# An expert layer's row gathers: half rows fetched by GpSimd against whole rows fetched by GpSimd and dealt out on chip by SyncE

## The chip, the core and the metric

The kernel runs on one core of a Trainium2 chip. The core has five engines with instruction lists of their own: TensorE (PE in the profile; PEld is its weight load), VectorE (DVE), ScalarE (ACT), GpSimd (POOL) and SyncE (SP), which here only issues transfers. They meet through semaphores. The metric is the device time of one execution in microseconds; less is better.

## The reference, cut to what matters

```python
def reference(x, w_r, w_i, b_r, b_i, moe):       # x: 8 x 1856 x 256
    X = np.fft.rfft(x, axis=1)
    Yr = soft_threshold(Xr @ w_r - Xi @ w_i + b_r, 0.01)
    Yi = soft_threshold(Xr @ w_i + Xi @ w_r + b_i, 0.01)
    y = np.fft.irfft(Yr + 1j * Yi, n=1856, axis=1)   # 14848 rows of 256
    # each row goes to one of 4 groups, and in it to one of 4 experts (argmax)
    for g, e in all 16 experts:
        h = np.maximum(y[rows of g, e] @ w1[g, e], 0)        # 256 x 1024
        out[rows of g, e] = (gate of the row) * (h @ w2[g, e])   # 1024 x 256
```

## The kernel before

The front part (transforms, threshold and routing, up to about 430 us) follows a long written order and isn't touched. It leaves the transformed rows y in DRAM as `ys_d` (one row of 256 floats, 1 KB, each) and for each expert a list of row numbers and gates in DRAM, `lst`.

The main part is a loop over 40 jobs. A job is up to 432 rows of one expert, in tiles of 128. Four experts ("fixed": 3, 1, 2 and 0) come at places known when the kernel is written; the other twelve come in the order of their size ("ranks" 0 to 11), which SyncE reads at run time from `order_r`. Ranks 1 to 9 have three jobs each, with the row counts in `CUTS`. The first four jobs fetch and transpose their rows on TensorE (`fetch`, `prep`). Jobs 4 to 39 are dealt:

- `deal` (from line 565) fills a tile `xm` (128 partitions x 4 tiles x 2 x 128 floats). It gathers half rows: for each tile and each half `b_` of its 128 rows one indirect transfer of 128 pieces of 512 B, by `half_ids`, row numbers doubled and arranged by eight small GpSimd computations for each 32-partition piece (L562). Partitions 64a to 64a+31 then hold the first halves of 32 rows, and the next 32 partitions their second halves.
- `turn_rows` transposes `xm` on VectorE in four instructions (L583) into `xtf`, and ScalarE and VectorE split that into two parts, `xth` (L589) and `xtl` (L590), whose sum keeps full accuracy in TensorE's fast format.
- `up_g` multiplies with w1 (L620, six matmuls for each of eight blocks), ScalarE takes the ReLU (`hh`, L625), VectorE the remainder (`hl`, L627).
- `down_g` multiplies with w2 (L693, L694), ScalarE and VectorE apply the gate (L698, L699; four buffers `yo`), and `store` sends each tile to its rows of `out` by an indirect transfer of GpSimd (L667).
- A new expert's weights come as two loads of 1 MB on SyncE into two buffers `xt` (L515), followed by the lists of its rows (L1105, L1107), in `dma_next`. `split_w` splits them piece by piece on ScalarE (L527) and VectorE (L528); the second load waits until a buffer has been split.

In iteration i the program is written in this order: down of job i-1 (two tiles), index computations of a new expert, `deal` of job i+2, up of job i with the pieces of a weight split, the loads of the next expert, `turn_rows` of job i+1, the rest of down of job i-1. GpSimd's list follows the program (`manual_schedule`); the other engines' lists are set by a scheduler.

Of the kernel before, what the change touches and what calls it, by code (L numbers as in the profile page):

```python
# [9 lines left out]
F32 = mybir.dt.float32  # L10
F32R = mybir.dt.float32r
BF16 = mybir.dt.bfloat16
I32 = mybir.dt.int32
AF = mybir.ActivationFunctionType
ALU = mybir.AluOpType
# [3 lines left out]
NB, S, D = 8, 1856, 256  # L19
# [5 lines left out]
NPAD = NP * PAIR  # L25
# [111 lines left out]
def spectral_moe(ctx: ExitStack, tc: tile.TileContext, x, wri, bri, wgate, w1, w1q, w2, cst, out):  # L137
    nc = tc.nc
# [6 lines left out]
    ys_d = dram.tile([NPAD + 1, D], F32, name="ys_d")  # L145
# [206 lines left out]
    def indices(ids, pool, both=True):  # L352
        if both:
            nc.gpsimd.tensor_copy(out=ids.gi, in_=ids.ent[:, :, 0])
        tmp = pool.tile([128, 12], F32, name="ixt", bufs=1)[:, 0:ids.n]
        nc.gpsimd.tensor_scalar(out=tmp, in0=ids.ent[:, :, 0], scalar1=0.0, scalar2=float(NPAD + 1), op0=ALU.is_equal, op1=ALU.mult)
        nc.gpsimd.tensor_scalar_add(out=tmp, in0=tmp, scalar1=-1.0)
        nc.gpsimd.tensor_tensor(out=tmp, in0=tmp, in1=ids.ent[:, :, 0], op=ALU.add)
        nc.gpsimd.tensor_copy(out=ids.si, in_=tmp)

    class Ids:
        def __init__(self, ent, gi, si):
            self.ent, self.gi, self.si, self.n, self.last = ent, gi, si, gi.shape[1], 128
            self.half = None

        def cut(self, a_, b_):
            part = Ids(self.ent[:, a_:b_], self.gi[:, a_:b_], self.si[:, a_:b_])
            if self.half is not None:
                part.half = self.half[:, a_:b_]
            if b_ == self.n:  # L370
                part.last = self.last
            return part
# [131 lines left out]
    with tc.issue_after(x1.ins):  # L504
        nc.sync.dma_start(out=lst[0:NE * CAP].rearrange("(e s) k -> e s k", e=NE)[:, 0:ZROWS].rearrange("e (j c) k -> e j (c k)", j=16),
                          in_=zero[0:NE, 0:ZROWS // 16].rearrange("p c k -> p (c k)").unsqueeze(1).broadcast_to([NE, 16, ZROWS // 8]))
# [44 lines left out]
            out_.append((xg, w, ids.rows(c0 + w - 1)))  # L551
        return out_

    half_rows = ys_d.rearrange("r (h d) -> (r h) d", h=2)

    def half_ids(ids, nm):
        ids.half = ft.tile([128, ids.n, 2], I32, name=f"half_{nm}")
        for a_ in range(2):
            for b_ in range(2):
                for h in range(2):  # L560
                    q, p = 64 * a_ + 32 * h, 64 * b_ + 32 * a_
                    nc.gpsimd.tensor_scalar(out=ids.half[q:q + 32, :, b_], in0=ids.ent[p:p + 32, :, 0], scalar1=2.0, scalar2=float(h),  # L562
                                            op0=ALU.mult, op1=ALU.add)

    def deal(ids):
        xm = xq.tile([128, 4, 2, 128], F32, name="xm")
        for c in range(ids.n):
            for b_ in range(2):
                left = ids.rows(c) - 64 * b_
                if left > 0:  # L570
                    m = 64 if left <= 32 else 128
                    nc.gpsimd.indirect_dma_start(  # L572
                        out=xm[0:m, c, b_, :], out_offset=None, in_=half_rows,
                        in_offset=bass.IndirectOffsetOnAxis(ap=ids.half[0:m, c, b_:b_ + 1], axis=0))
        return xm.rearrange("p c b d -> p (c b) d")

    def turn_rows(xm, ids):
# [516 lines left out]
    first, xp2 = [], None  # L1094
# [43 lines left out]
    by_hand = ExitStack()  # L1138
# [16 lines left out]
        assert not (sorts or moved or turns or parked) and all(next(g, None) is None for c, g in steps.items() if c not in "SNOP")  # L1155
        wts = {e: views(w) for e, w in wts.items()}
    inv.close()
    by_hand.enter_context(tc.manual_schedule(engines={mybir.EngineType.Pool}))

    xq = ctx.enter_context(tc.tile_pool(name="xq", bufs=2, reuse_waits="tile"))  # L1160
    hq = ctx.enter_context(tc.tile_pool(name="hq", bufs=2, reuse_waits="tile"))
# [201 lines left out]
    def ranked(k):  # L1363
        return nc.values_load(order_r[:, k:k + 1], engines=sp, min_val=0, max_val=NE - 1)

    def halves(parts, ids):
        c = 0
        for p in parts:
            p.half = ids.half[:, c:c + p.n]
            c += p.n  # L1370
        return parts

    def rank_ids(k, ek):
        rows = CUTS[k]
        n = sum((m + 127) // 128 for m in rows)
# [56 lines left out]
    def dma_next(i):  # L1432
        if not loads:
            return
        j = loads.pop(0)
        kind, q = jobs[j]
        if kind == "l":
            raws[j] = raw_w(q[0], w1q)
        else:
            k = q[0]  # L1440
            ek = ranked(k)
            raws[j] = raw_w(ek, w1q)
            rids[k], whole = rank_ids(k, ek)
            ready[i + 2] = lambda: (indices(whole, ft), half_ids(whole, f"r{k}"), halves(rids[k], whole))

    table = flex_table()
    for j, (kind, q) in enumerate(jobs):
# [11 lines left out]
            indices(fids[e][0], ft, False)  # L1459

    ready[0] = fixed_ids
    ready[3] = lambda: (half_ids(fids[0][0], "f0"), halves(fids[0][1], fids[0][0]))
    for i, (kind, q) in enumerate(jobs):
        ids = jids[i]
        if kind == "r":
# [49 lines left out]
    next(rest)  # L1515
    drain(behind_)
    drain(rest)
    by_hand.close()

    nfx = nc.values_load(nflex[:, 0:1], min_val=0, max_val=128)  # L1520
    with tc.For_i(KF, nfx, 1) as iv:
        rw, ids = flex_load(bass.ds(iv, 1))
        wt, todo = split_w(rw)
        emit(todo, len(todo))
        hts, hs = [], h_tiles()
        drain(flex_mm(prep(xq, fetch(xp2, ids, 3), 128), wt, hts))
        for q in range(2):
            flex_tr(hts[q], q, hs)
        down(psy, "py", hs, ids, wt, None, range(1))
        wt, ids = half_load(bass.ds(iv, 1))  # L1530
        hts, h = [], hq.tile([128, 8, WIDE], F32, name="hh")
        drain(half_mm(half_prep(fetch(xp2, ids, 3)), wt, hts))
        for q in range(2):
            half_tr(hts[q], q, h)
        half_down(h, ids, wt, None)
# [40 lines left out]
```

## Time and profile before

| what | value |
|---|---|
| median of 3 runs | 1128.2 us (1123.73 to 1131.09) |
| the profiled execution | 1122.3 us, span 1120.4 us |
| mean granted TensorE clock | 0.972 |
| TensorE busy | 1044.0 us (93%) |
| VectorE, ScalarE, GpSimd busy | 742.5, 486.4, 539.8 us |

The span runs from the first to the last instruction; the execution's time has 1.9 us around it. Times in the trace count from the span's start. "PEclk" is the TensorE clock granted, 1.00 being 2.4 GHz. SyncE's issuing of transfers is not counted as busy time.

### The profile page before, as it was taken

The page shows a single profiled execution, that of the slowest core. Times are in us where ns is not written, and L with a number is a line of the kernel's source. Part 1 is how long each engine was busy: PE and PEld are TensorE (multiplying, and loading weights), DVE is VectorE, ACT ScalarE, POOL GpSimd, SP SyncE. Part 2 cuts the span into 40 slices and gives each one's busy share as a digit, 9 for nine tenths or more (in the row PEclk, how much of TensorE's full clock was granted, in tenths as well). Part 3 has the DMA queues.
Part 4 walks back from the last instruction along what each step waited for, and adds up shares of the span by engine and source line. Part 5 has one row for each costly group of instructions (what it writes and reads, how often), then busy time and mean ns, then how long its engine had stood idle before and what let it go on. Part 6 is the DMA issues. An engine that isn't in the chain of part 4 may idle for free.

```text
span 1120.4 us, 24666 instructions
## 1 busy us (share of the span) xinstructions
PE 1044.0 (93%) x9496; PEld 897.6 (80%) x9496; DVE 742.5 (66%) x1754; ACT 486.4 (43%) x1273; POOL 539.8 (48%) x792
## 2 busy tenths in 40 slices
PE   8999999999999989898997999989899999997996
PEld 4886767767768878897896988878798888986896
DVE  6879999999897744462664757465575666655552
ACT  2664546437544333251443445243453544433442
POOL 0210255463764685644364554655365664463722
PEclk9999999999999999998998999999899999998989
DMA  9403314404135212312322223131322322223100
GB/s 386 120 2 131 135 40 153 151 5 153 49 127 183 81 58 58 123 64 75 100 80 88 85 69 117 42 126 45 104 85 70 128 65 94 78 86 98 48 30 28
DMA packets 34698, 105.32 MB, mean 94 GB/s; under 512 B 15052, under 2 KB 15769, under 8 KB 28050
## 3 DMA queue, kind: packets, MB, share of 16 engines
q1 hardware_dynamic: 16338, 55.92, 14.4%
q0 software_dynamic: 13344, 30.79, 9.2%
q10 hardware_dynamic: 4896, 17.01, 3.9%
q8 instruction: 76, 1.25, 0.5%
q14 instruction: 44, 0.36, 0.1%
HBM read 71.37 MB, written 32.46 MB: 93 GB/s over the span
## 4 chain that ended last, share of the span: by engine, by line
PE 62%; DVE 15%; issue 10%; POOL 6%; ACT 3%; DMA 3%; another core or an unknown queue 2%; ACTq 0%; POOLq 0%; SPq 0%; DVEq 0%
PE ph L620 21%; PE py L693 9%; PE py L694 5%; PE pw L885 5%; PE py L715 5%; PE ph L1045 3%; PE pw L867 2%; PE bank L909 2%; DMA big<-in_x_dram 2%; PE bank L927 2%; PE bank L803 2%; POOL xm L572 2%; PE bank L438 2%; POOL out_dram L667 1%
## 5 line engine op out<-in xcount | busy, mean ns | idle before, releaser
L620 PE MATMUL ph<-xth,big 128*128 128x256 f32 (+8 forms) x1280 | 298.1, 316 | 17.1 <-DVE hl L627 8.5
L627 DVE SCALAR_TENSOR_TENSOR hl<-ph,hh 128x256 fp32r<-128x256 f32 (+8 forms) x528 | 169.3, 355 | 176.2 <-ACT hh L625 110.9
L625 ACT ACTIVATE hh<-ph 128x256 fp32r<-128x256 f32 (+8 forms) x528 | 152.5, 337 | 222.6 <-PE ph L620 141.7
L620 PEld LDWEIGHTS ph<-xth,big 128*128 128x128 f32 x1280 | 220.4, 191 | 23.3 <-issue 12.5
L693 PE MATMUL py<-big,hh 128*128 128x512 f32 (+2 forms) x608 | 223.6, 405 | 8.3 <-ACT hh L625 4.4
L572 POOL DMA_INDIRECT xm<-ys_d,half_r x176 | 172.7, 981 | 68.3 <-issue 48.2
L620 PE MATMUL ph<-xtl,big 128*128 128x256 f32 (+8 forms) x640 | 201.6, 315 | 3.3 <-DVE xtl L590 2.9
L667 POOL DMA_INDIRECT out_dram<-yo,si_r x92 | 93.0, 1011 | 210.2 <-DVE yo L699 174.7
L694 PE MATMUL py<-big,hl 128*128 128x256 f32 (+2 forms) x608 | 175.3, 288 | 3.8 <-DVE hl L627 2.2
L693 PEld LDWEIGHTS py<-big,hh 128*128 128x128 f32 (+2 forms) x608 | 116.0, 191 | 37.2 <-ACT hh L625 6.2
L620 PEld LDWEIGHTS ph<-xtl,big 128*128 128x128 f32 x640 | 122.3, 191 | 6.3 <-DVE xtl L590 4.9
L694 PEld LDWEIGHTS py<-big,hl 128*128 128x128 f32 (+2 forms) x608 | 115.9, 191 | 9.6 <-DVE hl L627 6.5
L715 PE MATMUL py<-hh,big 128*128 128x320 f32 (+4 forms) x320 | 79.4, 327 | 9.0 <-issue 8.6
L851 POOL TENSOR_TENSOR xdl<-xd,xdh 128x512 fp32r<-128x512 f32 (+1 forms) x23 | 28.0, 1219 | 108.4 <-ACT xdh L844 88.1
L583 DVE STREAM_TRANSPOSE xtf<-xm 64x384 f32<-64x384 f32 (+3 forms) x144 | 72.8, 506 | 1.5
L589 ACT CAST xth<-xtf 128x512 fp32r<-128x512 f32 (+5 forms) x59 | 28.4, 517 | 101.4 <-DVE xtf L583 93.1
L528 DVE TENSOR_TENSOR big<-xt,big 128x512 fp32r<-128x512 f32 x104 | 70.9, 682 | 0.9 <-issue 0.2
L885 PE MATMUL pw<-wh,xh 128*128 128x256 f32 x240 | 66.5, 299 | 2.8 <-DVE pw L875 2.6
L715 PEld LDWEIGHTS py<-hh,big 128*128 128x128 f32 x320 | 57.9, 199 | 9.9 <-issue 8.4
L527 ACT CAST big<-xt 128x512 fp32r<-128x512 f32 x104 | 65.3, 627 | 0.0
L885 PE MATMUL pw<-wl,xh 128*128 128x256 f32 x240 | 62.0, 280 | 0.0
L890 ACT ACTIVATE big<-pw,nlam 128x512 f32<-128x512 f32 x60 | 41.4, 690 | 46.6 <-PE pw L885 45.7
(265 smaller groups left out, 2021.6 us busy)
## 6 DMA issues: line engine op xcount, KB each, us to landing
xt<-in_w_dram SPq DMA_DIRECT2D x21, 1024.0 KB
ys_d<-ysb ACTq DMA_DIRECT2D x32, 512.0 KB
xt<-in_w1q_dram SPq DMA_DIRECT2D x13, 1024.0 KB
big<-in_x_dram SPq DMA_DIRECT2D x8, 1024.0 KB
xt<-in_x_dram SPq DMA_DIRECT2D x8, 1024.0 KB
xm<-ys_d,half_r POOLq DMA_INDIRECT x176
out_dram<-yo,si_r POOLq DMA_INDIRECT x92
CI<-in_cst_dram SPq DMA_DIRECT2D x1, 1088.0 KB
```

The source lines that it names most:

```text
L527: nc.scalar.copy(out=wt[:, 2 * i, cs], in_=raws[i][:, cs])
L528: nc.vector.tensor_tensor(out=wt[:, 2 * i + 1, cs], in0=raws[i][:, cs], in1=wt[:, 2 * i, cs].bitcast(F32), op=ALU.subtract)
L572: nc.gpsimd.indirect_dma_start(out=xm[0:m, c, b_, :], out_offset=None, in_=half_rows, in_offset=bass.IndirectOffsetOnAxis(ap=ids.half[0:m, ...
L583: nc.vector.transpose(out=xt[64 * to:64 * to + 64, :, 0:k, 32 * a_:32 * a_ + 32].rearrange("f b c t -> f c b t"), in_=xm[64 * a_:64 * a_ + ...
L620: nc.tensor.matmul(o[:, :n], lhsT=a_[:, ch, fs], rhs=b_[:, ch, 0:n], start=k == 0, stop=k == 5)
L625: nc.scalar.activation(out=hh[:, f, cs], in_=o[:, cs], func=AF.Relu)
L627: nc.vector.scalar_tensor_tensor(out=hl[:, f, cs], in0=o[:, cs], scalar=0.0, in1=hh[:, f, cs].bitcast(F32), op0=ALU.max, op1=ALU.subtract)
L667: ins = nc.gpsimd.indirect_dma_start(out=out, out_offset=bass.IndirectOffsetOnAxis(ap=ids.si[0:ids.rows(t), t:t + 1], axis=0), in_=ysb, in ...
L693: nc.tensor.matmul(o, lhsT=hh[:, f, ts], rhs=w2b[:, :, f, :], start=f == 0, stop=f == 7, skip_group_check=True)
L694: nc.tensor.matmul(o[:, 0:D], lhsT=hl[:, f, ts], rhs=w2h[:, f, :], start=False, stop=f == 7, skip_group_check=True)
L715: nc.tensor.matmul(o, lhsT=w_[:, f, ds_], rhs=h_[:, f, 0:n], start=f == 0 and h_ is hh and w_ is w2h, stop=f == 7 and h_ is hh and w_ is n ...
L885: ins = nc.tensor.matmul(y, lhsT=a_[:, h, k % 2, j], rhs=t[:, j, h], start=False, stop=a_ is xl and h == 1, skip_group_check=True)
```

## The change

`deal` now gathers whole rows: GpSimd issues one indirect transfer for each tile into `xg` (three buffers of two tiles each). SyncE then copies from `xg` to `xm` on chip: for each pair of tiles, each 32 rows and each half of the row's columns one transfer of 32 partitions x 512 B (for one tile) or 1 KB (two tiles). A job of 384 rows takes 16 such transfers, and all jobs together 434. The index computations for half rows go. SyncE's list, like GpSimd's, now follows the program, and the load of `nflex` is written before that region ends.

```diff
-    def half_ids(ids, nm):
-        ids.half = ft.tile([128, ids.n, 2], I32, name=f"half_{nm}")
...
     def deal(ids):
         xm = xq.tile([128, 4, 2, 128], F32, name="xm")
-        for c in range(ids.n):
+        for c0 in range(0, ids.n, 2):
+            w = min(2, ids.n - c0)
+            xg = xp2.tile([128, 2, D], F32, name="xg", bufs=3)
+            for c in range(w):
+                m = -(-ids.rows(c0 + c) // 32) * 32
+                nc.gpsimd.indirect_dma_start(
+                    out=xg[0:m, c, :], out_offset=None, in_=ys_d[0:NPAD + 1, :],
+                    in_offset=bass.IndirectOffsetOnAxis(ap=ids.gi[0:m, c0 + c:c0 + c + 1], axis=0))
             for b_ in range(2):
-                left = ids.rows(c) - 64 * b_
-                if left > 0:
-                    m = 64 if left <= 32 else 128
-                    nc.gpsimd.indirect_dma_start(
-                        out=xm[0:m, c, b_, :], out_offset=None, in_=half_rows,
-                        in_offset=bass.IndirectOffsetOnAxis(ap=ids.half[0:m, c, b_:b_ + 1], axis=0))
+                for a_ in range(2):
+                    p = 64 * b_ + 32 * a_
+                    k = sum(ids.rows(c0 + c) > p for c in range(w))
+                    for h in range(2 if k else 0):
+                        q = 64 * a_ + 32 * h
+                        nc.sync.dma_start(out=xm[q:q + 32, c0:c0 + k, b_, :], in_=xg[p:p + 32, 0:k, 128 * h:128 * h + 128])
...
-    by_hand.enter_context(tc.manual_schedule(engines={mybir.EngineType.Pool}))
+    by_hand.enter_context(tc.manual_schedule(engines={mybir.EngineType.Pool, mybir.EngineType.SP}))
...
-            ready[i + 2] = lambda: (indices(whole, ft), half_ids(whole, f"r{k}"), halves(rids[k], whole))
+            ready[i + 2] = lambda: indices(whole, ft)
...
+
+    nfx = nc.values_load(nflex[:, 0:1], min_val=0, max_val=128)
     by_hand.close()
-
-    nfx = nc.values_load(nflex[:, 0:1], min_val=0, max_val=128)
```

GpSimd's list at rank 1's first deals (jobs 9 and 10), before; `half_r` are the computed half-row numbers, `out` rows are stores, and "x6" is six instructions alike:

```order
L562 TENSOR_SCALAR half_r_7824<-ent_r_7557 32x9 x8
L572 DMA xm<-ys_d,half_r_7824 128x128 x6
L1379 MEMSET ent_r_7951 128x18
L667 DMA out_dram<-yo,si_r_6544 16384x256
L667 DMA out_dram<-yo,si_f_176 16384x256 x2
L572 DMA xm<-ys_d,half_r_7824 128x128 x6
L667 DMA out_dram<-yo,si_f_176 16384x256 x2
```

After:

```order
L558 DMA xg<-ys_d,gi_r_7590 128x256 x3
L1365 MEMSET ent_r_7996 128x18
L660 DMA out_dram<-yo,si_r_6544 16384x256
L660 DMA out_dram<-yo,si_f_176 16384x256 x2
L558 DMA xg<-ys_d,gi_r_7590 128x256 x3
L660 DMA out_dram<-yo,si_f_176 16384x256 x2
```

The eight computations are gone, and each six gathers became three; the stores stand where they stood.

SyncE's list at the loads of rank 2, before (rows ISA set registers for the row behind them):

```order
L1107 ISA
L1107 DMA ent_r_7557<-lst 64x2
L1364 TENSOR_LOAD order_r
L1364 ISA x2
L515 ISA
L515 DMA xt<-in_w1q_dram 128x2048
L515 ISA
L515 DMA xt<-in_w_dram 128x2048
L1105 ISA
L1105 DMA ent_r_7951<-lst 128x6
L1105 ISA
L1105 DMA ent_r_7951<-lst 128x6
```

After:

```order
L567 DMA xm<-xg 32x2x128 x16
L567 DMA xm<-xg 32x128 x8
L1357 TENSOR_LOAD order_r
L1357 ISA x2
L512 ISA
L512 DMA xt<-in_w1q_dram 128x2048
L512 ISA
L512 DMA xt<-in_w_dram 128x2048
L1098 ISA
L1098 DMA ent_r_7996<-lst 128x6
L1098 ISA
L1098 DMA ent_r_7996<-lst 128x6
```

The deals of jobs 8 and 9 now stand ahead of the weight loads, and those of jobs 10, 11 and 12 behind the lists; here is that end of the lists, after:

```order
L1100 ISA
L1100 DMA ent_r_7996<-lst 32x2
L567 DMA xm<-xg 32x2x128 x8
L567 DMA xm<-xg 32x128 x8
L567 DMA xm<-xg 32x2x128 x8
L567 DMA xm<-xg 32x128 x4
L567 DMA xm<-xg 32x2x128 x8
L567 DMA xm<-xg 32x128 x8
```

Nothing stood between these lists and the next expert's loads before; now 44 transfers do.

## Rows read from the trace of the kernel before

**Rows 1.** The page: busy us, share and instructions of each engine.

```profile
PE 1044.0 (93%) x9496; PEld 897.6 (80%) x9496; DVE 742.5 (66%) x1754; ACT 486.4 (43%) x1273; POOL 539.8 (48%) x792
```

**Rows 2.** Windows with a low clock: us, busy of each engine, PEclk, DMA, GB/s.

```profile
512.00:530.00 18.00, 13.49 (x48) 11.08 (x47) 2.66 (x11) 2.70 (x9) 6.14 (x7) 0.72 0.10 26
590.00:612.00 22.00, 15.78 (x85) 12.94 (x84) 9.27 (x27) 5.61 (x14) 10.70 (x12) 0.77 0.21 60
776.00:796.00 20.00, 15.34 (x72) 13.95 (x71) 11.41 (x29) 8.45 (x25) 7.23 (x7) 0.83 0.29 90
900.00:932.00 32.00, 29.53 (x171) 26.18 (x171) 20.78 (x49) 14.75 (x40) 16.62 (x28) 0.95 0.32 104
996.00:1022.00 26.00, 19.41 (x98) 17.54 (x97) 9.51 (x27) 6.90 (x23) 13.91 (x16) 0.80 0.25 76
1056.00:1072.00 16.00, 12.05 (x54) 11.02 (x53) 6.09 (x19) 4.00 (x16) 4.75 (x5) 0.79 0.10 25
sum 134.00, PE 105.59 PEld 92.70 DVE 59.72 ACT 42.41 POOL 59.35; mean PE 17.60 PEld 15.45 DVE 9.95 ACT 7.07 POOL 9.89
```

**Rows 3.** The same view of thirteen other windows: one and the sum.

```profile
932.00:996.00 64.00, 62.52 (x430) 58.24 (x430) 39.85 (x94) 27.76 (x75) 34.40 (x58) 1.00 0.24 73
...
sum 419.00, PE 402.31 PEld 371.61 DVE 252.23 ACT 180.85 POOL 216.52; mean PE 30.95 PEld 28.59 DVE 19.40 ACT 13.91 POOL 16.66
```

**Rows 4.** Waits: engine, line, releaser, us in total, times, longest.

```profile
ACT hh L625 <- remote: 48.7, 19, 4.6
```

**Rows 5.** Windows of six GpSimd runs, first and last: L572 alone, then L667.

```profile
498.30:520.10 21.80, 11.86 (x12) 0.95 0.46 152
...
1044.20:1062.10 17.90, 10.72 (x11) 1.00 0.21 56
...
498.30:520.10 21.80, 4.88 (x5) 0.95 0.46 152
...
1044.20:1062.10 17.90, 2.98 (x3) 1.00 0.21 56
```

**Rows 6.** Timeline of ScalarE: start, us, instruction, idle before and its releaser.

```profile
601.79 0.38 ACT L625 ACTIVATE hh<-ph 128x256 fp32r<-128x256 f32 x1 [3.85 <-remote]
```

**Rows 7.** Timeline of TensorE there.

```profile
606.45 0.79 PE L693 MATMUL py<-big,hh 128*128 128x512 f32 x1 [3.18 <-ACT hh L625]
```

**Rows 8.** Timeline of GpSimd in a run of ten: first and last two.

```profile
951.50 1.07 POOL L572 DMA_INDIRECT xm<-ys_d,half_r  x1 [0.28 <-POOL half_r L562]
...
962.30 0.94 POOL L572 DMA_INDIRECT xm<-ys_d,half_r  x1 [0.30 <-issue]
963.55 0.94 POOL L572 DMA_INDIRECT xm<-ys_d,half_r  x1 [0.30 <-issue]
```

**Rows 9.** Timeline of SyncE at the fixed experts' lists: first and last of nine.

```profile
429.30 0.81 SPq L1105 DMA_DIRECT2D ent_f<-lst  x2
...
432.50 0.89 SPq L1105 DMA_DIRECT2D ent_f<-lst  x2
```

**Rows 10.** Timeline of GpSimd behind these lists.

```profile
431.84 1.01 POOL L546 DMA_INDIRECT xg<-ys_d,gi_f  x1 [0.72 <-DMA ent_f<-lst]
```

**Rows 11.** Chain of waits between 870 and 890 us, in order of time.

```profile
877.66 5.19 DMA xm<-ys_d,half_r
```

**Rows 12.** Timeline of GpSimd: first gathers of two jobs.

```profile
702.00 1.00 POOL L572 DMA_INDIRECT xm<-ys_d,half_r  x1 [0.30 <-issue]
...
889.96 0.99 POOL L572 DMA_INDIRECT xm<-ys_d,half_r  x1 [0.30 <-issue]
```

**Rows 13.** Timeline of VectorE: the turns of these two jobs.

```profile
721.87 2.32 DVE L583 STREAM_TRANSPOSE xtf<-xm 64x384 f32<-64x384 f32 x4
...
907.28 1.73 DVE L583 STREAM_TRANSPOSE xtf<-xm 64x384 f32<-64x384 f32 x3
```

**Rows 14.** Timeline of SyncE: a second weight load.

```profile
609.35 0.33 SPq L515 DMA_DIRECT2D xt<-in_w_dram  x1
```

**Rows 15.** Timeline of VectorE: the turn that follows it.

```profile
622.96 2.32 DVE L583 STREAM_TRANSPOSE xtf<-xm 64x384 f32<-64x384 f32 x4
```

More of the change, by code (lines that the diff above doesn't have):

```diff
@@ L363, in __init__ @@
             self.ent, self.gi, self.si, self.n, self.last = ent, gi, si, gi.shape[1], 128
-            self.half = None
         def cut(self, a_, b_):
             part = Ids(self.ent[:, a_:b_], self.gi[:, a_:b_], self.si[:, a_:b_])
-            if self.half is not None:
-                part.half = self.half[:, a_:b_]
             if b_ == self.n:
@@ L552, in fetch @@
         return out_
-    half_rows = ys_d.rearrange("r (h d) -> (r h) d", h=2)
-    def half_ids(ids, nm):
-        ids.half = ft.tile([128, ids.n, 2], I32, name=f"half_{nm}")
[L558 to L563, printed above, removed]
     def deal(ids):
         xm = xq.tile([128, 4, 2, 128], F32, name="xm")
-        for c in range(ids.n):
-            for b_ in range(2):
-                left = ids.rows(c) - 64 * b_
-                if left > 0:
-                    m = 64 if left <= 32 else 128
-                    nc.gpsimd.indirect_dma_start(
-                        out=xm[0:m, c, b_, :], out_offset=None, in_=half_rows,
-                        in_offset=bass.IndirectOffsetOnAxis(ap=ids.half[0:m, c, b_:b_ + 1], axis=0))
+        for c0 in range(0, ids.n, 2):
[6 more added lines that the diff above has]
+                    in_offset=bass.IndirectOffsetOnAxis(ap=ids.gi[0:m, c0 + c:c0 + c + 1], axis=0))
+            for b_ in range(2):
+                for a_ in range(2):
[4 more added lines that the diff above has]
+                        nc.sync.dma_start(out=xm[q:q + 32, c0:c0 + k, b_, :], in_=xg[p:p + 32, 0:k, 128 * h:128 * h + 128])
         return xm.rearrange("p c b d -> p (c b) d")
@@ L1364, in ranked @@
         return nc.values_load(order_r[:, k:k + 1], engines=sp, min_val=0, max_val=NE - 1)
[L1366 to L1371, printed above, removed]
     def rank_ids(k, ek):
@@ L1461, in spectral_moe @@
     ready[0] = fixed_ids
-    ready[3] = lambda: (half_ids(fids[0][0], "f0"), halves(fids[0][1], fids[0][0]))
     for i, (kind, q) in enumerate(jobs):
```

## The prediction

> **What bounds the kernel now.** I read the page's busy table first: TensorE is busy 1044.0 us of the 1120.4 us span [rows 1]. So only two things can shorten this kernel without less arithmetic: TensorE's idle time, and time at its lower clock. I then cut the main part (from about 510 us on) into stretches and read TensorE's busy time and granted clock in each. Thirteen stretches, 419 us in all, have a granted clock of 1.00 throughout and TensorE busy 402.31 us, so 4% idle [rows 3]. Six others, 134 us in all, have only 105.59 us busy and a clock of 0.72 to 0.95 [rows 2]. A mean of 0.72 is a mixture of the two levels, full and half (2.4 and 1.2 GHz).
>
> What those six cost: idle is 134.00 - 105.59 = 28.4 us, and 4% idle would be 5.3, so 23 us are excess. The clock takes the sum of (1 - clock) x length: 5.0 + 5.1 + 3.4 + 1.6 + 5.2 + 3.4 = 23.7 us; TensorE was busy 79% of that time, so some 19 us are really lost. Together **42 us**, lost in 134 us.
>
> What ends the idle time? The wait list has 48.7 us in 19 waits of ScalarE's ReLU (L625) with the releaser "remote", that is, one the profile doesn't see [rows 4]. The timeline of one such place shows the chain: ScalarE's ReLU at 601.79 comes after 3.85 us of idleness, although the up matmul that it reads had ended; TensorE's down matmul at 606.45 then waits 3.18 us for the next such ReLU [rows 6, 7]. Something holds back the hand-over from TensorE to ScalarE.
>
> What else runs there? GpSimd: all six stretches begin inside a long run of indirect transfers that GpSimd issues without a pause. Six such runs lie there; by line they hold 12, 12, 9, 8, 11 and 11 gathers (L572) and 5, 3, 3, 2, 5 and 3 stores (L667), so 17, 15, 12, 10, 16 and 14 transfers (first and last row of each in [rows 5]). The late ReLUs begin five or more us after a run's start, and I found none over 1 us late outside or just behind a run. Runs of at most 6 transfers hurt almost nothing. A run of ten from 951.50 to 964.49 [rows 8] lies in a stretch where TensorE was busy 62.52 of 64.00 us at full clock [rows 3]. The mechanism is not visible in these views; the coincidence is, and I build on it.
>
> **The change, part by part.**
>
> *Gathers.* 184 half-row gathers become 96 whole-row ones of the same kind, so each saves one of the 1.3 us steps at which they follow each other in [rows 8]. GpSimd's 104 small index computations (L562) go too. GpSimd's own time is worth nothing: TensorE never waits for its sum. What counts is the length of the runs. With the same stores, and 12, 12, 9, 8, 11, 11 gathers made into 6, 6, 5, 4, 6, 6, the six runs become 11, 9, 8, 6, 11 and 9 transfers. The order of GpSimd's rows around the second run shows 6, 3 and 6 turn into 3, 3 and 3. Before, the 12-run's stretch (776 to 796) lost 20 - 15.34 - 0.8 = 3.9 us idle and some 2.6 us of clock, so 6.5 [rows 2]; the 10-run in rows 8 lost next to nothing, that in 900 to 932 about 2.5. So I price a run of 11 at 5 us, of 8 or 9 at 1, of 6 at nothing: 5 + 1 + 0 + 0 + 5 + 1 = **12 us stay of 42, 30 go**. From outside: none may go (0), or all 42 and some 5 of the 16.7 us idle in rows 3 (47).
>
> *The transfers on SyncE.* 434 transfers of 16 or 32 KB are added to SyncE, which has little else to do. A job's 384 rows need 16 of them. No such transfer is in the trace. The nearest is the burst of nine list loads, the first issued at 429.30 and the last pair at 432.50 [rows 9], so seven steps in 3.2 us, 0.46 each; single ones are 0.47 apart, which I take. How long one takes to land: the gather at 431.84 was released by a list load [rows 10], and its load went out about 430.15, so 1.7 us; the longest landing in the chain of waits is 5.19 us [rows 11]. From the first gather to the turn of a job the new path needs 2 gathers (2.6) + landing 1.7 + 16 x 0.47 (7.5) + landing 1.7 = 13.5 us. What is there now: the gathers of one such job start at 702.00 and VectorE turns its rows at 721.87, so 19.9 us; the tightest job has 889.96 to 907.28, so 17.3 [rows 12, 13]. Five jobs have 16 transfers and so little room, four of them about 20 us. So 4 to 6 us are to spare and the term is 0. It decides when the spacing passes (19.9 - 6.0) / 16 = 0.87 us, or 0.71 in the tightest job. At an upper bound taken from the 5.19 us landing spread over eight transfers in flight (0.65 us; in the order each waits for the eighth before it) the path is 2.6 + 1.7 + 10.4 + 5.2 = 19.9 and only the tightest job is late, by 2.6 us.
>
> *SyncE's order is now as written.* A deal stands behind the weight loads of the job before it where the code says so, and the second weight load waits for the splitting of the weights before. One such place in the trace: that load goes out at 609.35, the four lists behind it take it to about 611.8 at 0.47 us each, and VectorE turns the rows at 622.96 [rows 14, 15]. After it 16 transfers take to 619.4 and land by 621.1, which is 1.9 us early; if a lane first waits for the 1 MB load, they land about a microsecond later. Three places are so built and two have less room. I charge **4 us** for them (0 to 8). The weight loads themselves come later by a deal, up to 8 us, and are still read much later.
>
> *The other edits* have one answer, nothing: the last loads move to the end of SyncE's list, and the orders of TensorE, ScalarE and VectorE are unchanged. Gathers now wait for one of three buffers; in the order, what frees it stands ahead of the weight load in SyncE's list.
>
> Sum against the profiled execution: 1122.3 - 30 + 4 = 1096.3 us. The median of the runs shown, 1128.2, is 5.9 above that execution, so I carry the difference: **1102 us**.
>
> **A rule that speaks against it.** The list loads go out 0.47 us apart while each lands after about 1.7 us, so several are in flight [rows 9, 10]. The Trainium skill ("DMA: Bandwidth & Descriptors", sections "Anatomy of one DMA — SWDGE (gpsimd) path" and "Rules for kernel authors") gives every transfer some 2.0 us of fixed cost, says that under 64 KB one pays mostly overhead and should coalesce, and that transfers to disjoint partition parts serialize. Read as one after the other, 434 of them would take some 900 us of SyncE, an estimate from that page, and the kernel would come out far slower. The lists in this trace do not behave so, but they are smaller than 16 KB.
>
> **The rivals.**
>
> *The stalls stay (within 1%).* If the late hand-over hangs on all small transfers in flight, and not on GpSimd's, then SyncE's 434 take the place of the 88 gathers that go. For: nothing in the trace shows the mechanism. Against: the releases are late only around GpSimd's runs, while the stretches of rows 3 hold most of the 1 MB weight loads and run at full clock. The gain of 30 goes, the 4 stay: 1126 in the profiled execution, **1132** as median. In the same page's section "SWDGE vs HWDGE vs iDMA" the Trainium skill has GpSimd write its descriptors by software while SyncE's are made in hardware; that would speak for GpSimd as the cause, and no row here shows it.
>
> *SyncE is too slow (slower).* One mechanism: the spacing of the 16 transfers passes 0.87 us and the turn on VectorE waits, with TensorE behind it. At GpSimd's own spacing of about 1.25 us, the step of its last two gathers [rows 8], a job's path is 2.6 + 1.7 + 20 + 1.7 = 26.0 us: four jobs come 6.1 us late, the tightest 8.7, so 33; other jobs with more room some 5. After each wait TensorE runs at half clock for a while, as in rows 2; 2 us each, so 10. 1122.3 - 30 + 4 + 48 = 1144, as median **1150**. Against it: the spacing in rows 9. Its far end is one transfer at a time, 16 x 1.7 = 27 us in place of 7.5, and a time of about 1185.
>
> *It doesn't do what it says (within 1%).* GpSimd's gathers wait for buffers that SyncE frees only after a weight load; the stores behind them on GpSimd wait too, their four buffers fill, and ScalarE and TensorE stand. Twelve experts' loads lie in this part; if six block so, at 5 us each, somewhat more than the waits in rows 6 and 7, the gain is used up: 1126, so **1132**. Against it: the order, in which three buffers reach past a weight load.
>
> **How the numbers follow.** Chances: the forecast 0.55 (its own range 1083 to 1117), the stalls stay 0.22, SyncE too slow 0.15, buffers 0.08. A difference of 1%, about 11 us, is what a measurement of this kernel can tell from none. Faster by over 1% is the forecast and a little more, 0.56; within 1% is the two middle cases less their tails, 0.27; slower 0.17. The range begins where all 42 us and a little more go (1083) and must take in the two cases at 1132 with the spread of the runs shown, so it ends at 1137; most of "SyncE too slow" is left out.
>
> **What would show it.** Right: the six stretches have a clock near 1.00 and TensorE idle near 4%, GpSimd's runs are 11 transfers at most, the waits "remote" of L625 fall from 48.7 us to under 15, SyncE's transfers follow each other at 0.4 to 0.6 us, and VectorE's turns don't wait for them. Wrong: late ReLUs while GpSimd is still, or in runs of 8 or 9; turns that wait for SyncE's transfers; or GpSimd's stores standing behind a gather that waits.

## The result and the profile after

| | before | after |
|---|---|---|
| median of the runs | 1129.6 us (1123.7 to 1137.0, 4 runs) | 1072.7 us (1071.2 to 1074.7, 4 runs) |
| the profiled execution | 1122.3 us | 1074.7 us |
| mean granted clock | 0.972 | 0.994 |

The ratio is 0.9494, 95% interval 0.9435 to 0.9554: 5.1% faster, where the forecast was 2.3% and the range went down only to 1083. The direction and the place were right, the size was not. And the runs showed something that the prediction doesn't contain at all: on three of the six chips that the experiments met, the kernel before takes only 1036 to 1037 us, and on the one of these three on which the changed kernel itself was timed, the change gains nothing.

The page's line on the engines, which answers to [rows 1]:

```profile
PE 1019.2 (95%) x9496; PEld 883.2 (82%) x9496; DVE 740.7 (69%) x1754; ACT 484.6 (45%) x1273; POOL 431.3 (40%) x600
```

TensorE does the same matmuls in 25 us less busy time, with less of it at half clock; GpSimd has lost 108 us. The windows of the same work as the six of [rows 2] (us, busy time of PE, PEld, DVE, ACT and POOL with their instructions, PEclk, DMA share, GB/s):

```profile
503.00:521.00 18.00, 18.00 (x103) 16.76 (x102) 9.81 (x27) 6.04 (x17) 5.84 (x7) 1.00 0.52 177
580.00:604.00 24.00, 22.06 (x135) 19.58 (x134) 14.59 (x43) 10.24 (x29) 10.81 (x15) 1.00 0.52 157
752.00:772.00 20.00, 19.76 (x117) 18.36 (x117) 14.39 (x37) 11.70 (x34) 6.39 (x7) 1.00 0.35 93
878.00:906.00 28.00, 27.10 (x171) 24.71 (x170) 20.28 (x48) 14.18 (x39) 10.34 (x11) 1.00 0.44 136
960.00:984.00 24.00, 23.03 (x155) 21.95 (x154) 14.90 (x39) 10.13 (x32) 13.19 (x14) 1.00 0.36 96
1012.00:1030.00 18.00, 18.00 (x105) 17.26 (x104) 10.47 (x28) 7.75 (x25) 1.02 (x1) 1.00 0.14 31
sum 132.00, PE 127.95 PEld 118.63 DVE 84.44 ACT 60.03 POOL 47.60; mean PE 21.33 PEld 19.77 DVE 14.07 ACT 10.01 POOL 7.93
```

In [rows 2] TensorE was busy 105.59 of 134 us at a clock of 0.72 to 0.95; now it is busy 127.95 of 132 at 1.00 in every window. Measured from one job's first up matmul to that of the next around each place, the six became 7.3, 7.6, 7.8, 4.4, 10.4 and 6.8 us shorter, 44 us together, of 47.6 between the two profiled executions. The rest of the main part became some 6 us shorter, and the untouched front part was 3.6 us longer in this execution. So the time went where the prediction looked for it.

The list of waits (engine, line, releaser: us in total, times, longest), which answers to [rows 4]:

```profile
ACT hh L618 <- remote: 19.9, 10, 4.1
POOL out_dram L660 <- DMA xm<-xg: 18.3, 6, 8.3
POOL xg L558 <- DMA xm<-xg: 18.1, 8, 9.3
```

Late ReLUs (L618, L625 before) have fallen from 48.7 us to 19.9, which is more than the 15 that I had set. The other two lines are new. Gathers wait eight times, 18.1 us in all, for buffers that SyncE's transfers empty. The waits of six stores are put down to SyncE's transfers too, but what each of these stores waits for itself is VectorE's counter, which says that its rows are ready (for the one at 583.60 below it stepped at 583.34); the SyncE steps that the profile names there belong to waits of the gather behind. GpSimd's timeline at the place that had 15 transfers in a row before (start, us, instruction, idle before and its releaser):

```profile
575.62 0.95 POOL L558 DMA_INDIRECT xg<-ys_d,gi_r  x1 [0.30 <-issue]
...
579.48 0.95 POOL L660 DMA_INDIRECT out_dram<-yo,si_r  x1 [2.79 <-DVE yo L692]
580.78 1.02 POOL L660 DMA_INDIRECT out_dram<-yo,si_f  x1 [0.35 <-DVE yo L692]
583.60 0.99 POOL L660 DMA_INDIRECT out_dram<-yo,si_f  x1 [1.81 <-DMA xm<-xg]
584.90 1.33 POOL L558 DMA_INDIRECT xg<-ys_d,gi_r  x1 [0.30 <-issue]
586.53 1.17 POOL L558 DMA_INDIRECT xg<-ys_d,gi_r  x1 [0.30 <-issue]
588.00 0.95 POOL L558 DMA_INDIRECT xg<-ys_d,gi_r  x1 [0.30 <-issue]
597.55 1.02 POOL L660 DMA_INDIRECT out_dram<-yo,si_f  x1 [8.61 <-DVE yo L692]
```

I had counted three gathers, three stores and three gathers in one run of nine. It falls into pieces of three, two and four: the first store waits 2.79 us for its rows, the third 1.81 us for its own, and the store behind the last gathers 8.61 us. GpSimd, with less to do, comes to its stores before their rows are ready, where it came late before and found everything waiting. No run in the main part is longer than eight, where I had counted 11. SyncE's timeline there shows 16 transfers:

```profile
577.28 11.23 SPq L567 DMA_DIRECT2D xm<-xg  x16
```

11.23 us for 16 is 0.70 us each, not 0.47 (over all 434 the median step is 0.64). That is under the 0.87 at which a usual job would be late and about at the 0.71 of the tightest; VectorE's turns (L576) waited for no transfer in this execution.

### The profile page after: what moved, and what is told of

Its sections match the earlier page's. It is cut to its first block, busy times and chain, and to the rows that moved or that the text cites. A ratio compares the mean times of both kernels' runs of the same rounds, so it can differ in the third digit from the quotient of the medians.

```text
span 1072.9 us, 25190 instructions
## 1 busy us (share of the span) xinstructions
PE 1019.2 (95%) x9496; PEld 883.2 (82%) x9496; DVE 740.7 (69%) x1754; ACT 484.6 (45%) x1273; POOL 431.3 (40%) x600
## 3 DMA queue, kind: packets, MB, share of 16 engines
q1 hardware_dynamic: 46450, 67.81, 19.9%
## 4 chain that ended last, share of the span: by engine, by line
PE 69%; DVE 15%; issue 5%; DMA 4%; POOL 3%; ACT 2%; SPq 1%; another core or an unknown queue 0%; ACTq 0%; DVEq 0%; POOLq 0%
PE ph L613 24%; PE py L686 10%; PE py L708 6%; PE pw L878 5%; PE py L687 5%; PE ph L1038 2%; PE pw L860 2%; PE bank L902 2%; PE bank L920 2%; DMA big<-in_x_dram 2%; PE bank L796 2%; PE bank L435 2%; DVE big L525 2%; DVE hl L620 1%; PE bank L1061 1%
## 5 line engine op out<-in xcount | busy, mean ns | idle before, releaser
L613 PE MATMUL ph<-xth,big 128*128 128x256 f32 (+8 forms) x1280 | 291.6, 311 | 2.5 <-ACT xth L582 1.6
L618 ACT ACTIVATE hh<-ph 128x256 fp32r<-128x256 f32 (+8 forms) x528 | 150.4, 336 | 189.2 <-PE ph L613 137.6
L613 PEld LDWEIGHTS ph<-xth,big 128*128 128x128 f32 x1280 | 216.7, 188 | 6.2 <-ACT xth L582 3.7
L686 PE MATMUL py<-big,hh 128*128 128x512 f32 (+2 forms) x608 | 218.9, 399 | 1.6 <-ACT hh L618 1.1
L613 PE MATMUL ph<-xtl,big 128*128 128x256 f32 (+8 forms) x640 | 199.4, 312 | 3.3 <-DVE xtl L583 2.8
L686 PEld LDWEIGHTS py<-big,hh 128*128 128x128 f32 (+2 forms) x608 | 113.7, 187 | 29.8 <-ACT hh L618 1.9
L687 PEld LDWEIGHTS py<-big,hl 128*128 128x128 f32 (+2 forms) x608 | 113.9, 187 | 10.4 <-DVE hl L620 9.7
L558 POOL DMA_INDIRECT xg<-ys_d,gi_r x92 | 91.9, 999 | 46.7 <-issue 28.6
L708 PE MATMUL py<-hh,big 128*128 128x320 f32 (+4 forms) x320 | 73.5, 313 | 4.9 <-issue 3.3
L576 DVE STREAM_TRANSPOSE xtf<-xm 64x384 f32<-64x384 f32 (+3 forms) x144 | 72.9, 506 | 1.7 <-issue 0.2
L708 PEld LDWEIGHTS py<-hh,big 128*128 128x128 f32 x320 | 54.5, 188 | 6.0 <-issue 3.7
```

Of the source, the lines that this page charges most:

```text
L558: nc.gpsimd.indirect_dma_start(out=xg[0:m, c, :], out_offset=None, in_=ys_d[0:NPAD + 1, :], in_offset=bass.IndirectOffsetOnAxis(ap=ids.gi[ ...
L576: nc.vector.transpose(out=xt[64 * to:64 * to + 64, :, 0:k, 32 * a_:32 * a_ + 32].rearrange("f b c t -> f c b t"), in_=xm[64 * a_:64 * a_ + ...
L613: nc.tensor.matmul(o[:, :n], lhsT=a_[:, ch, fs], rhs=b_[:, ch, 0:n], start=k == 0, stop=k == 5)
L618: nc.scalar.activation(out=hh[:, f, cs], in_=o[:, cs], func=AF.Relu)
L686: nc.tensor.matmul(o, lhsT=hh[:, f, ts], rhs=w2b[:, :, f, :], start=f == 0, stop=f == 7, skip_group_check=True)
L687: nc.tensor.matmul(o[:, 0:D], lhsT=hl[:, f, ts], rhs=w2h[:, f, :], start=False, stop=f == 7, skip_group_check=True)
```

## The experiments

Lines of the ReLU and of the stores move by a few in these kernels. Each ratio is against the kernel before on the same chip. The experiments met six chips. On three the kernel before takes 1130 to 1134 us, as in the runs of the result (whose chip the record doesn't name); on the other three it takes 1036 to 1037. I call them chips with and without late hand-overs, for a reason that follows. Each chip was met in one round of runs only, so that the chip decides, and not something else that differs from round to round, is read from six rounds and not tested.

**SyncE's order alone** (with late hand-overs), in the kernel before:

```diff
-tc.manual_schedule(engines={mybir.EngineType.Pool})
+tc.manual_schedule(engines={mybir.EngineType.Pool, mybir.EngineType.SP})
```

> The kernel before, with SyncE's list in program order as in the changed kernel, and nothing else. Theory 'run length' and theory 'pieces': within 1% of 1128. Theory 'SyncE's order' (weight and list loads at better places make the gain): 1095 or less.

1133.9 against 1133.9 us, ratio 1.000 (0.996 to 1.005). The order of SyncE's list is not the gain.

**The same gathers as before, with SyncE's transfers** (with late hand-overs), in the changed kernel:

```diff
-    out=xg[0:m, c, :], in_=ys_d[0:NPAD + 1, :], ap=ids.gi[0:m, ...]
+    for h in range(2):
+        out=xg[0:m, c, 128 * h:128 * h + 128], in_=half_rows, ap=ids.half[0:m, c0 + c, h:h + 1]
```

> The changed kernel, but GpSimd fetches each tile into xg as two gathers of half rows (as many gathers and as small pieces as in the kernel before; index computations for them, two per list); SyncE's transfers and order as changed. Theory 'run length' (ReLUs are late while GpSimd issues indirect transfers without a pause for more than some 5 us; late ones add up in runs of ten and more until TensorE stands): runs of 12 to 16 transfers return and the time goes back to 1105 to 1130 us, with half-clock stretches again. Theory 'SyncE's order': stays within 1% of 1073. Theory 'pieces' (the number of 512 B pieces fetched from DRAM): also back to 1105 to 1130, whatever the runs look like.

1172.1 us, ratio 1.031 (1.022 to 1.039): not only the gain is gone, it is slower than before. SyncE's order is refuted as the cause a second time; 'run length' and 'pieces' both said 1105 to 1130, and neither said 1172. The waits:

```profile
ACT hh L630 <- remote: 85.5, 24, 12.1
```

85.5 us in 24 waits, the longest 12.1. GpSimd has runs of 16 transfers again, and SyncE's work on top.

**The index work put back** (with late hand-overs), in the changed kernel: the 104 computations of L562, their results unused.

```diff
-ready[i + 2] = lambda: indices(whole, ft)
+ready[i + 2] = lambda: (indices(whole, ft), half_ids(whole, f"r{k}"))
```

> The changed kernel with the 104 index computations for half rows put back on GpSimd, their results unused. Theory 'run length': within 1% of 1073, since they issue no transfer. Theory 'index work' (these GpSimd computations hold up VectorE or ScalarE): 20 us or more slower.

1085.1 us, 12 more than the changed kernel of the first runs: neither expectation. The trace says where: up to the start of job 34 it is some 4 us behind the changed kernel, and then it loses 10 us in one place. There the index work had made GpSimd late, its gathers and stores met, and 13 transfers followed each other. GpSimd, the first of them, the last, and the next transfer after the pause:

```profile
965.34 1.08 POOL L567 DMA_INDIRECT xg<-ys_d,gi_r  x1 [0.28 <-POOL half_r L557]
...
980.77 0.95 POOL L567 DMA_INDIRECT xg<-ys_d,gi_r  x1 [0.30 <-issue]
985.80 1.21 POOL L567 DMA_INDIRECT xg<-ys_d,gi_r  x1 [4.07 <-DMA xm<-xg]
```

TensorE, the end of the second block's up matmuls (with the first of the third), the last matmul before it stands, and the next:

```profile
971.73 0.45 PE L622 MATMUL ph<-xth,big 128*128 128x320 f32 x2
...
976.20 0.31 PE L622 MATMUL ph<-xth,big 128*128 128x320 f32 x1
985.69 0.61 PE L622 MATMUL ph<-xth,big 128*128 128x320 f32 x1 [9.18 <-DVE hl L629]
```

ScalarE, the ReLUs of the first two blocks:

```profile
974.16 0.50 ACT L627 ACTIVATE hh<-ph 128x256 fp32r<-128x256 f32 x2 [2.37 <-PE ph L622]
984.46 0.50 ACT L627 ACTIVATE hh<-ph 128x256 fp32r<-128x256 f32 x2 [9.80 <-remote]
```

The second block's matmuls end at about 972; ScalarE waits for nothing else, as its list shows a wait for TensorE's counter alone, and gets the release 12 us later, 2.7 us after GpSimd's last transfer. The trace's record of that counter shows the same: no step between 974.13 and 984.43, then five within half a microsecond. TensorE meanwhile runs out of buffers for its results and stands for 9.18 us. From ScalarE to VectorE and on to TensorE the hand-over is prompt (984.46 + 0.50, then 985.69 behind VectorE): only what TensorE hands over comes late. So it is over the whole trace of the kernel before: behind 440 us, 61 steps of TensorE's counter come more than 1 us after the last matmul that makes one, and none of ScalarE's, VectorE's and GpSimd's, the program's last two steps set aside. The case above is one clean case of the mechanism that the coincidences in the kernel before had suggested.

**Pauses everywhere** (with late hand-overs), in the kernel before, ahead of every second tile of a deal:

```diff
+            if c % 2 == 0:
+                for _ in range(10):
+                    nc.gpsimd.memset(idle, 0.0)
```

> The kernel before, with a pause of ten small GpSimd memsets (128 x 256, some 2 to 3 us together) ahead of every second tile of each deal, so that no run of indirect transfers is longer than about 8; as many half-row gathers and pieces as before, and each of them later. Theory 'run length': the six stalls go, 1080 to 1105 us. Theory 'pieces': no gain, 1128 or, as deals and stores come later, up to 1145. Theory 'earlier stores' (the gain is that stores no longer stand behind gathers): slower than 1128.

1142.0 us, ratio 1.007 (1.004 to 1.010). By its time 'run length' has failed here. The waits show two things at once:

```profile
ACT yo L739 <- DMA out_dram<-yo,si_r: 57.3, 8, 11.5
ACT yo L701 <- DMA out_dram<-yo,si_r: 25.5, 8, 9.3
ACT hh L628 <- remote: 4.4, 3, 2.4
```

The late ReLUs are gone (4.4 us against 48.7) with as many gathers and pieces as before. In their place ScalarE waits 83 us for buffers `yo` whose stores stand behind the pauses on GpSimd. One wait was exchanged for another; my price had left out that GpSimd has no 3 us to spare in each half deal. 'Earlier stores' had said slower, and so it was; that the stores' place is not the gain is decided by the last experiment below, where pauses ahead of each deal make a kernel faster.

**One pause for each rank**, in the kernel before:

```diff
             ahead[i + 2] = deal(jids[i + 2])
+            if new:                      # a rank's first deal, and one fixed expert's
+                for _ in range(10):
+                    nc.gpsimd.memset(idle, 0.0)
```

> The kernel before with a pause of some 3.4 us (ten GpSimd memsets) only behind the first deal of each rank, so in 13 places; it cuts each long run of indirect transfers there into about 6 and 9, and moves what follows by 3.4 us. Theory 'run length': most of the six stalls go and the waits of the ReLU with an unseen releaser fall from some 50 to 70 us to 25 or less; 1085 to 1110 us. Theory 'work done on GpSimd' (the kernel before is slow because GpSimd has too much to do and stores stand behind it): 1130 to 1160.

1043.4 us against 1036.5 (1.003 to 1.009): this is a chip on which the kernel before takes 1036. No ReLU is late there, even behind 18 transfers in a row (606.70 to 629.36). Two repetitions:

> The kernel before with 13 pauses of 3.4 us on GpSimd behind the first deal of each rank, once more. Theory 'late hand-over in long runs': on a chip where the kernel before takes about 1130, 1085 to 1110 and 25 us or less of ReLU waits with an unseen releaser; on the other kind of chip 1043 as before.

> The kernel before with 13 pauses of 3.4 us behind the first deal of each rank, a third time, in the hope of a chip that shows late hand-overs: there 1085 to 1110 by the theory 'run length', 1130 or more if the number of transfers decides.

Both met chips without late hand-overs: 1042.4 and 1042.9, ratios 1.004 and 1.007. The fourth met one with:

> The kernel before with 13 pauses once more, for a chip that shows late hand-overs: 1085 to 1110 by 'run length', 1130 or more if the number of transfers decides. On a chip that shows none, 1043.

1114.9 against 1133.0, ratio 0.984 (0.975 to 0.994; two runs against three). That is a gain, as 'run length' said and 'number' did not, but less than its 1085 to 1110: many runs of eight to twelve are left, with 28.3 us of late ReLUs.

**The changed kernel on other chips.**

> The changed kernel itself, once more. The runs so far were made on two chips: on one the kernel before takes about 1130 us, on the other about 1036 us and no ReLU is late, even behind 17 indirect transfers in a row. Theory 'late hand-over' (the change gains only by what the late hand-overs cost): where the kernel before takes about 1130 this takes about 1073 again; where it takes about 1036 this takes 1033 to 1043, no gain. Theory 'the change saves work': a ratio of 0.95 on every chip.

1040.6 against 1037.5 us, ratio 1.002 (1.000 to 1.004). It gains nothing here, as the theory 'late hand-over' said. The whole main part (440 to 1035 us, columns as above) of the kernel before, of the changed kernel, and of this run, in this order:

```profile
440.00:1035.00 595.00, 551.59 (x3336) 501.63 (x3334) 343.67 (x911) 244.32 (x712) 313.20 (x454) 0.96 0.27 86
```

```profile
440.00:1035.00 595.00, 574.04 (x3585) 530.95 (x3584) 369.88 (x983) 264.42 (x777) 230.78 (x298) 1.00 0.37 110
```

```profile
440.00:1035.00 595.00, 588.52 (x3742) 554.66 (x3740) 383.36 (x1014) 279.03 (x806) 242.78 (x305) 1.00 0.37 111
```

TensorE idle for 43, 21 and 6.5 us of the 595. And the kernel before on a chip without late hand-overs (with the one pause for each rank, the trace there is nearest to it):

```profile
440.00:1035.00 595.00, 589.07 (x3746) 555.44 (x3746) 383.31 (x1015) 278.75 (x806) 389.97 (x625) 1.00 0.28 91
```

5.9 us idle. The trace of the changed kernel on this kind of chip also shows what the change itself costs, at VectorE's turn of job 10 behind the weight load of rank 2:

```profile
595.66 1.16 DVE L576 STREAM_TRANSPOSE xtf<-xm 64x384 f32<-64x384 f32 x2 [2.39 <-DMA xm<-xg]
```

It waits 2.39 us, and TensorE stands 2.27 us and runs 3.4 us at half clock.

> The changed kernel itself, beside the other: 1065 to 1080 on a chip with late hand-overs, 1040 on one without.

1076.3 against 1130.5, ratio 0.953 (0.947 to 0.959), on another chip with late hand-overs. So the changed kernel itself was timed three times: two gains of 5% where hand-overs are late, no gain on the one chip where they are not. On the other chips only kernels derived from it were timed.

**What on GpSimd does it: transfers, pieces or time.** In the changed kernel, behind one deal in each of nine iterations:

```diff
             ahead[i + 2] = deal(jids[i + 2])
+            if i % 3 == 0 and 9 <= i <= 33:      # m = 128, or 16, or 15 memsets instead
+                for c in range(6):
+                    nc.gpsimd.indirect_dma_start(out=burst[0:m, c, :], in_=quarter rows of ys_d, ap=jids[i + 2].gi[0:m, 0:1])
```

> The changed kernel with six more indirect gathers (128 rows of 256 B, into a tile that nobody reads) right behind one deal in each of nine iterations, so that runs there grow to some 10 to 14. Theory 'run length': ReLUs come up to 10 us late there as in the kernel before, TensorE stands and drops to half clock; 1095 to 1130 us. Theory 'GpSimd time': as the same time spent in memsets, within 10 us of that kernel.

> The changed kernel with 15 memsets (some 7 us) on GpSimd in the same nine places instead of the six gathers. Theory 'run length': 1070 to 1085, no late ReLUs but perhaps a wait for stores. Theory 'GpSimd time': as slow as the kernel with gathers.

> The changed kernel with six more indirect gathers of only 16 rows each in the same nine places. If the number of pieces that GpSimd writes out holds the hand-over up: an eighth of the effect, 1070 to 1080. If each indirect transfer counts, whatever its size: as with 128 rows, 1095 to 1130, since GpSimd takes about as long for each.

1046.0, 1046.4 and 1045.1 us against 1036.5: one chip without late hand-overs, and all three cost the same, so there the kind of work makes no difference. The first of them again:

> The changed kernel with six more indirect gathers in each of nine places, once more. Theory 'late hand-over': on a chip where the kernel before takes about 1130, late ReLUs, TensorE standing and half clock at most of the nine places, 1095 to 1130; on the other kind of chip 1045 as before, that is some 5 to 10 us over the changed kernel.

1047.4 against 1037.5, such a chip again; the changed kernel took 1040.6 on it. Then all three kinds in one kernel, in turn, so that one run tells them apart:

> The changed kernel with three kinds of extra GpSimd work in the same nine places, in turn: six indirect gathers of 128 rows (from the jobs 9, 18 and 27 on), 15 memsets (12, 21, 30), six indirect gathers of 16 rows (15, 24, 33). On a chip that shows late hand-overs: theory 'transfers without a pause' has TensorE late or standing behind both kinds of gathers and not behind the memsets; theory 'pieces written out' behind the gathers of 128 rows alone; theory 'GpSimd busy' behind all three. On a chip that shows none: 1045, alike in all places.

1047.4 against 1036.8: no late hand-overs there either. And on a chip with them:

> The kernel with mixed extra work once more, for a chip that shows late hand-overs; the theories expect of it what they expected before: late ReLUs and standing behind both kinds of gathers, not behind memsets ('transfers without a pause'), behind the 128-row gathers alone ('pieces'), behind all three ('GpSimd busy'). On a chip that shows none, 1045.

1109.1 against 1133.0, so some 35 us slower than the changed kernel on such chips. The nine places in order, 25 us from each on; the kinds in turn are 128 rows, memsets, 16 rows:

```profile
604.00:629.00 25.00, 16.21 (x83) 14.65 (x82) 11.03 (x27) 9.19 (x28) 11.59 (x13) 0.86 0.28 67
654.00:679.00 25.00, 25.00 (x146) 23.82 (x145) 16.30 (x43) 13.74 (x43) 16.31 (x26) 1.00 0.23 63
703.00:728.00 25.00, 22.39 (x121) 20.01 (x120) 14.32 (x33) 10.79 (x30) 16.17 (x17) 0.86 0.25 69
755.00:780.00 25.00, 22.18 (x121) 19.84 (x120) 14.52 (x37) 11.45 (x32) 13.52 (x14) 0.93 0.22 58
798.00:823.00 25.00, 24.00 (x155) 22.12 (x153) 13.15 (x31) 10.53 (x30) 18.07 (x31) 1.00 0.30 80
847.00:872.00 25.00, 20.48 (x118) 18.52 (x117) 12.27 (x29) 9.42 (x26) 12.20 (x13) 0.86 0.16 44
901.00:926.00 25.00, 21.94 (x116) 19.73 (x116) 16.07 (x40) 10.38 (x31) 11.83 (x13) 0.93 0.23 58
943.00:968.00 25.00, 25.00 (x175) 24.30 (x174) 16.53 (x42) 11.10 (x34) 18.10 (x31) 1.00 0.29 79
983.00:1008.00 25.00, 19.48 (x106) 18.00 (x104) 10.84 (x29) 7.55 (x24) 16.62 (x19) 0.80 0.23 66
```

Behind the memsets TensorE is idle 0.0, 1.0 and 0.0 us at full clock. Behind the gathers of 128 rows it is idle 8.8, 2.8 and 3.1 us, behind those of 16 rows 2.6, 4.5 and 5.5, with a clock of 0.80 to 0.93 in all six. The memsets of one place take 7.1 us, six gathers about 7.5. Nor is it the places: over the same 18 to 32 ReLUs each, and compared with the two traces of the changed kernel on chips with late hand-overs, the work became 4.0 to 9.9 us longer behind gathers of 128 rows, 2.4 to 11.7 behind those of 16 rows, and between 3.0 shorter and 1.2 longer behind memsets. So GpSimd's time alone does nothing, and an eighth of the pieces does as much: each indirect transfer counts, whatever its size.

**Run length or number**, in the changed kernel, where GpSimd has time to spare:

```diff
+            for _ in range(10):
+                nc.gpsimd.memset(idle, 0.0)
             ahead[i + 2] = deal(jids[i + 2])
```

> The changed kernel with a pause of some 3.1 us (ten memsets) on GpSimd ahead of each deal, so that hardly a run has more than 5 indirect transfers. On a chip that shows late hand-overs theory 'run length' has the ReLU's waits with an unseen releaser under 8 us (19.9 in the changed kernel) and a time of 1050 to 1065, faster than both kernels; its rival 'number of transfers' has no gain, 1073 or more. On a chip that shows none: 1040 to 1048.

1059.3 against 1036.8 us on a chip without late hand-overs, 19 us over the changed kernel on another such chip: more than expected, the pauses make deals late. On a chip with them, beside the changed kernel itself:

> The changed kernel with a pause ahead of each deal once more, for a chip that shows late hand-overs. 'Run length': 1050 to 1070 there, below the changed kernel. If only the number of transfers counted: 1080 or more, the changed kernel plus the some 20 us that the pauses cost on a chip without late hand-overs. On such a chip: 1059.

1066.2 us, ratio 0.944 (0.937 to 0.951), and 1076.3 for the changed kernel, two runs each. The waits with the pauses, and then without:

```profile
ACT hh L618 <- remote: 1.0, 1, 1.0
```

```profile
ACT hh L618 <- remote: 14.7, 8, 6.2
```

The same transfers with pauses between them: the late ReLUs are gone, and the kernel is 10 us faster though the pauses cost 19 elsewhere. What holds the hand-over up is the unbroken run, not the number; and SyncE's 434 transfers, which are all in this kernel, do not. As a kernel it is no improvement: it wins on one kind of chip and loses 2% on the other.

## Why the prediction was wrong in size

*What bounds the kernel: right.* The late hand-over from TensorE inside GpSimd's runs was the cause; the bursts and the pauses show it. The 42 us were about right for the six places, too. Cut into jobs, the kernel before is 44.7 us longer there than the same kernel with one pause for each rank on a chip without late hand-overs. What I did not see is that the reference was itself disturbed: all other stretches are 32.3 us longer. The trace could have told. Only 5 of the 19 late ReLUs of [rows 4] lie in the windows of [rows 2], while 11 lie in those of [rows 3], which I took as normal; two of them, both in runs of eight:

```profile
807.04 0.47 ACT L625 ACTIVATE hh<-ph 128x256 fp32r<-128x256 f32 x2 [2.39 <-remote]
...
851.53 0.47 ACT L625 ACTIVATE hh<-ph 128x256 fp32r<-128x256 f32 x2 [2.35 <-remote]
```

The change took only 6 of these 32 us, so they are not where the forecast missed. Between the two kinds of chips the kernel before differs by 1129.6 - 1036.5 = 93 us; that all of it is late hand-over is not shown, 77 is what the two traces compared here differ by in the jobs.

*"12 us stay of 42, 30 go": the step that failed.* All of it went, 44 us in the six places. I kept GpSimd's order, halved its gathers and took it that GpSimd would still issue everything without a pause, which gave runs of up to 11. (By my own prices the third run, of eight, should also have cost 1 us, so 13 and not 12.) In the trace no run is over eight, mostly because GpSimd, with less to do, now waits for the rows of its stores, and at a few places for SyncE's transfers. I had priced waits of GpSimd only as a rival that loses time; here they helped. My own sign of being wrong, late ReLUs in runs of eight, did show: 10 are left, 19.9 us, in runs of five to eight.

*The miss in numbers.* Forecast and result are 29 us apart: 14 are this term (44 for 30), 7 the 4 us that I charged for SyncE and that did not come, with small gains elsewhere, and 8 the carrying to the median below.

*The transfers on SyncE: right that they cost nothing, spacing mis-sized.* It is 0.64 to 0.70 us, not 0.47. It stayed under the 0.87 that I had worked out, and the tightest job with its 0.71 was closer than I thought.

*Deals behind weight loads: charged, and not seen in the result.* I charged 4 us for three places. On the chip without late hand-overs one of them shows, 2.3 us of standing and 3.4 us at half clock; the median there is 3 us higher (1040.6 against 1037.5), which the interval (1.000 to 1.004) hardly tells from nothing. In the trace of the result it doesn't show.

*Carrying the profiled execution to the median.* I added 5.9 us. Before's execution (1122.3) lies below all its runs, 7 us under their median, but after's lies 2 us above its own, so the 5.9 should have been -2.0. That is scatter of single executions, not the change.

*The rivals.* "The stalls stay" is refuted by [rows 2] against the windows after, and by the changed kernel with pauses, where SyncE's 434 transfers leave 1.0 us of late ReLUs. "SyncE is too slow" did not come. Buffers on GpSimd did make waits, 18 us of them, and the gain stood all the same. The rule of the Trainium skill ("DMA: Bandwidth & Descriptors", "Rules for kernel authors") that transfers to disjoint partition parts serialize is not borne out as the prediction read it, one after the other at 2 us each: 16 such transfers went out in 11.23 us, 0.70 us apart. The 2 us, moreover, stand on that page as a fit for transfers that GpSimd issues, not SyncE.

*Not in the prediction:* that the gain depends on the chip. Nothing in one chip's trace told it. What on the chip delays TensorE's releases, and why only on three of six, stays open; the runs tell only what triggers it. One rival is untested: the traces from chips with late hand-overs also hold fewer records of semaphore steps (of ScalarE's counter 910 to 1023, against 1131 to 1147 on the others), and every experiment's execution on record comes with its span and granted clock. Whether the recording takes part in the delay, or an execution without it is as late, no run tells.

## What to carry to other kernels

When a wait has no visible releaser, look at what another engine does at that time, and then test that by adding the suspected work in a few places of one kernel and an equal time of harmless work in others. Do not take a kernel's own quiet stretches as undisturbed. And time a change on more than one chip before you believe a gain that comes from a stall: this one is worth 5% where hand-overs come late and nothing on the chip where they do not.

## What the runs showed of the hardware

- On three chips of six, while GpSimd issues indirect transfers about 1.3 us apart without a pause, releases from TensorE reach ScalarE late (and VectorE: 17.0 us in 8 waits in the kernel before). In runs of five to twelve ScalarE waited mostly 1 to 5 us for one (9.1 at most), the earliest 5.7 us after the run's first transfer; the longest waits were 9.8 to 12.7 us, in runs of 13 to 16. Transfers of 16 rows do it as those of 128 do (TensorE idle 12.6 and 14.7 us in three places each); memsets (1.0 us), SyncE's transfers and runs broken by pauses of 3 us (1.0 us of late ReLUs against 14.7) do not.
- The same kernel took 1130 to 1134 us on these chips and 1036 to 1037 on the others.
- After TensorE had stood, for 1 to 9 us in one piece or in several, its granted clock was at half (1.2 GHz) for 3.4 to 10 us in the traces of the kernel before and after, and for up to 20 us in the kernel with half-row gathers and SyncE's transfers.
- On-chip transfers of 16 to 32 KB from SyncE followed each other at 0.64 us (median) to 0.70 us.
